# Weight conversion with its first step in an attention PSUM bank, its checks in later blocks, and q in hp's bank for block 0

## The chip, the cores and the metric

One core of one Trainium2 chip runs the whole program. The metric is the time of one execution on the device in microseconds (us); for the kernel before it is the median of three runs. Engine names as in the profile: PE is TensorE, PEld its weight load, DVE VectorE, ACT ScalarE, POOL GpSimd, SP SyncE, whose queue issues the DMAs here.

## The reference

All inputs are float64. First a recurrent attention over 768 time steps for 4 x 8 heads of width 48, then two feed-forward layers over the 3072 tokens that result (384 wide):

```python
for t in range(S):                                   # attention, state is D x D
    cur = einsum('bhd,bhe->bhde', u[None] * kt, vt)
    y[:, :, t] = einsum('bhd,bhde->bhe', rt, state + cur)
    state = wt[:, :, :, None] * state + einsum('bhd,bhe->bhde', kt, vt)
x = y.transpose(0, 2, 1, 3).reshape(B * S, H * D)
h = x @ w_in;  x = (h - tanh(h)) @ w_out             # first layer, d_ff 2048
h = x @ w_in2; e = exp(h - max(h)); sm = e / (sum(e) + 1e-9)
out = (layernorm(h * sm) * g_ln) @ w_out2            # second layer, d_ff 1024
```

## The kernel before

The attention works in chunks of 128 time steps: 24 units (4 batches of 6 chunks), each in stages att_pre and att_0 to att_4. A unit's r, k, w and v come by four DMAs of 192 KB (att_load); TensorE transposes them (tp), VectorE forms running products of w (inc, L201) and decayed keys (kh, L214 and L215), TensorE multiplies qk, kt, ds and y. Stages of unit u need the state st of unit u-1 (L254, L255). The result y goes as a pair of tiles, a rounded value and its remainder, into xs, six small DMAs from x3 included.

The first layer (part1, part2) works on blocks of 512 tokens, six blocks, each of 16 steps m over d_ff. In a step part1 multiplies hp (9 matmuls of 128 x 512, since both operands are split in a rounded part and a remainder), then t = hp squared (ScalarE, L315), y = hp * t (VectorE, L316), q (ScalarE, L317), y = (q + const) * y (VectorE, L319), a range check of t (ScalarE, L320), and g in two parts on GpSimd: rounding (L321) and remainder (L322). part2 adds g of two steps ago into the three x2p banks (9 matmuls). Block i needs the units 4i to 4i+3; four units of the next block are worked in between the steps. The second layer's h and o matmuls follow, after block 5.

The weights arrive as float64 bit patterns: a raw tile of 128 x 2 x 384 pairs of words holds a pair, 128 columns of w_in and 128 rows of w_out (768 KB). convert makes float32 of it: ScalarE scales the low words (L118); VectorE shifts and masks the high words (L119, a one-input operation on 768 elements), ors in the sign (L120) and adds the low part (L121); ScalarE rounds (L124), GpSimd takes the remainder (L125); then ScalarE checks the high words with two passes (L127 and L128, in place, so the raw tile comes free only behind them). There are 16 pairs of the first layer (raw_a, conv_a, due before step m of block 0) and 8 of the second (raw_b, conv_b, in block 5). Raw tiles have two buffers, cv_x too.

PSUM: three banks x2p, two banks "h" for hp, three banks "a" for the attention's tiles (in units 0 to 3 the h and x2p banks serve too). A pool's buffers are handed out in the order in which the code asks for them. The code is written in the order of the loops, and a scheduler then sets the order of each engine's instructions by its own estimates; within an engine they run in that order. fast_path puts two conv_a between the first four units, and conv_a of pair s + 2 into step s:

```python
first += [(2.0 * m, lambda m: K.conv_a(cv, cvr, m), m) for m in range(early)]
...
        if 0 <= s < NM - early:
            K.conv_a(cv, cvr, s + early)
```

Of the kernel before, what the change touches and what calls it, by code (L numbers as in the profile page):

```python
# [55 lines left out]
class Kern:  # L56
# [49 lines left out]
    def like(self, a, out):  # L106
        return a if len(out.shape) == 2 else a.rearrange("p (j f) -> p j f", j=out.shape[1])

    def convert(self, pool, raw, hi, lo, col, scale=None):

        nc, v = self.nc, self.nc.vector
        flat = raw.rearrange("p i f two -> p (i f) two")
        H_, L_ = flat[:, :, 1], flat[:, :, 0]
        x = pool.tile([128, 2 * DM], U32, tag="cv_x", name="cv_x")
        xf = x.bitcast(F32)
        nc.scalar.activation(L_, L_, AF.Copy, scale=2.0**-29)  # L118
        v.tensor_scalar(x, H_, 3, 0x3FFFFFF8, ALU.logical_shift_left, ALU.bitwise_and)  # L119
        v.scalar_tensor_tensor(x, H_, 0xC0000000, x, ALU.bitwise_and, ALU.bitwise_or)  # L120
        v.tensor_tensor(x, x, L_, ALU.add)  # L121
        if scale is not None:
            nc.scalar.activation(xf[:, DM:], xf[:, DM:], AF.Copy, scale=scale)
        nc.scalar.copy(hi, xf)  # L124
        nc.gpsimd.tensor_tensor(lo, xf, hi, ALU.subtract)  # L125
        Hf = H_.bitcast(F32)
        nc.scalar.activation(Hf, Hf, AF.Square)  # L127
        nc.scalar.activation(Hf, Hf, AF.Relu, bias=self.c_flag, scale=-1.0, accum_out=self.flags[:, col:col + 1])  # L128


    def att_setup(self, att, xp0, xp1):
# [164 lines left out]
        return raw  # L296

    def conv_a(self, pool, rpool, m):
        raw = rpool.tile([128, 2, DM, 2], U32, tag="raw", name="raw_a")
        self.load_w1(raw[:, 0], m)  # L300
        self.load_w2(raw[:, 1], m)
        self.convert(pool, raw, self.wa[:, 0, m], self.wa[:, 1, m], 2 * NU + NB * NM + m)

    def part1(self, i, m):
        nc, v, g = self.nc, self.nc.vector, self.nc.gpsimd
        hp = self.ps_h.tile([128, BLK], F32, tag="h", name="hp")
        xs = self.xs[i % 2]
        seq = [(a, b, j) for j in range(KM) for a, b in ((1, 0), (0, 1), (0, 0))]
        for n, (a, b, j) in enumerate(seq):
            self.mm(hp, self.wa[:, a, m, j * 128:(j + 1) * 128], xs[:, b, j], start=n == 0, stop=n == len(seq) - 1)  # L310
        t = self.gp.tile([128, BLK], F32, tag="t", name="t")
        q = self.gp.tile([128, BLK], F32, tag="q", name="q")
        y = self.gp.tile([128, BLK], F32, tag="y", name="y")
        gs = self.gs.tile([128, 2, BLK], F32R, tag="g", name="g")
        nc.scalar.activation(t, hp, AF.Square)  # L315
        v.tensor_tensor(y, hp, t, ALU.mult)  # L316
        nc.scalar.activation(q, t, AF.Square, bias=self.c_fsb, scale=F_S)  # L317
        col = 2 * NU + i * NM + m
        v.scalar_tensor_tensor(y, q, F_E, y, ALU.add, ALU.mult)  # L319
        nc.scalar.activation(q, t, AF.Relu, bias=self.c_t2, accum_out=self.flags[:, col:col + 1])  # L320
        g.tensor_scalar(gs[:, 0], y, 1.0, 1.0, ALU.mult, ALU.mult)  # L321
        g.tensor_tensor(gs[:, 1], y, gs[:, 0], ALU.subtract)  # L322
        return gs

# [36 lines left out]
        return raw  # L361

    def conv_b(self, pool, rpool, k):
        raw = rpool.tile([128, 2, DM, 2], U32, tag="raw", name="raw_b")
        self.load_w3(raw[:, 0], k)
        self.load_w4(raw[:, 1], k)
        self.convert(pool, raw, self.wb[:, 0, k], self.wb[:, 1, k], 2 * NU + NB * NM + NM + k, self.gl[:, k:k + 1])
# [92 lines left out]
def fast_path(tc, K, const):  # L460
    nc = tc.nc
# [280 lines left out]
```

## Time and profile before

| what | value |
|---|---|
| runs of the kernel before | 842.88, 843.4, 844.35 us; median 843.4 |
| profiled execution | 843.12 us |
| its span, first to last instruction | 841.3 us |
| mean granted TensorE clock | 0.972 |
| busy, share of the span | PE 92%, PEld 77%, DVE 65%, ACT 58%, POOL 48% |
| DMA | 55.43 MB, 66 GB/s in the mean |

The span falls into the start (attention units 0 to 3 and the first conversions, up to the first hp matmul at 79.3 us), block 0 (up to about 193 us), blocks 1 to 4, block 5 with the second layer's conversions (from about 526 us), and the second layer (from 614 us). Shares of busy time are means over these; a stage has to be read by itself.

### The profile page before, as it was taken

To read this page: it belongs to the slowest core of one execution; us is meant where nothing else is said; L and a number is where in the kernel's file an instruction comes from. 1 tells how busy PE (TensorE), PEld (TensorE's weight loads), DVE (VectorE), ACT (ScalarE), POOL (GpSimd) and SP (SyncE) were. 2 spreads that over 40 slices of the span, in tenths; PEclk is the share of its full clock that TensorE was granted. 3 is DMA by queue.
4 is the path that set the end of the run, shared out by engine and by line. 5 is a ranking of instruction groups with operands and counts; after the bars stand their busy time and mean duration, and the time that the engine had idled before them with its cause. 6 is when DMAs were issued, how large, how long until landed. Compare 5 with 4: busy or idle time off the path is not lost.

```text
span 841.3 us, 13250 instructions
## 1 busy us (share of the span) xinstructions
PE 773.4 (92%) x4706; PEld 646.9 (77%) x4706; DVE 550.4 (65%) x949; ACT 486.0 (58%) x912; POOL 406.4 (48%) x376
## 2 busy tenths in 40 slices
PE   5556598899999999999999999989989999999996
PEld 3545476688888888888888888767869999999996
DVE  4968798967655566555556555585376667666763
ACT  4655778856555655565556555687545454444442
POOL 4645487866556555556565554668412111111110
PEclk9876899999999999999999999999999999999999
DMA  9976547443222222232132000230011111111100
GB/s 162 172 164 131 124 117 155 105 93 81 43 44 43 71 51 36 41 80 44 33 51 71 16 6 24 80 113 10 1 56 48 39 47 38 48 48 39 48 29 33
DMA packets 137484, 55.43 MB, mean 66 GB/s; under 512 B 105792, under 2 KB 132032, under 8 KB 137408
## 3 DMA queue, kind: packets, MB, share of 16 engines
q1 hardware_dynamic: 137408, 54.49, 28.7%
q8 instruction: 39, 0.64, 0.3%
q14 instruction: 37, 0.30, 0.1%
HBM read 42.67 MB, written 9.44 MB: 62 GB/s over the span
## 4 chain that ended last, share of the span: by engine, by line
PE 77%; DVE 7%; DMA 5%; issue 3%; SPq 3%; ACT 3%; POOL 2%; DVEq 0%; ACTq 0%; POOLq 0%
PE x2p L329 20%; PE hp L310 20%; PE o L431 12%; PE h L386 11%; PE tp L192 3%; PE qk L228 3%; PE tt L420 2%; DMA raw_a<-in_moe_w_out_dram 2%; PE y L270 2%; PE y L267 2%; DVE cv_x L119 1%; SPq L161 1%; PE kt L234 1%; DVE cv_x L120 1%; DVE y L319 1%
## 5 line engine op out<-in xcount | busy, mean ns | idle before, releaser
L329 PE MATMUL x2p<-g,wa 128*128 128x512 f32 x864 | 223.8, 399 | 10.9 <-POOL g L322 9.5
L310 PE MATMUL hp<-xs,wa 128*128 128x512 f32 x864 | 226.1, 402 | 4.4 <-DVE y L316 4.4
L329 PEld LDWEIGHTS x2p<-g,wa 128*128 128x128 f32 x864 | 159.7, 189 | 48.0 <-POOL g L322 12.7
L310 PEld LDWEIGHTS hp<-xs,wa 128*128 128x128 f32 x864 | 163.4, 192 | 42.4 <-DVE y L316 7.1
L321 POOL TENSOR_SCALAR g<-y 128x512 fp32r<-128x512 f32 x96 | 71.1, 740 | 132.4 <-DVE y L319 122.7
L322 POOL TENSOR_TENSOR g<-y,g 128x512 fp32r<-128x512 f32 x96 | 131.1, 1366 | 7.3
L316 DVE TENSOR_TENSOR y<-hp,t 128x512 f32<-128x512 f32 x96 | 66.0, 689 | 93.1 <-ACT t L315 77.1
L320 ACT ACTIVATE q<-t,cst 128x512 f32<-128x512 f32 x96 | 69.6, 725 | 78.6 <-DVE y L319 78.4
L431 PE MATMUL o<-wb,ts 128*128 128x384 f32 x576 | 110.1, 341 | 2.1 <-DVE st L400 1.1
L386 PE MATMUL h<-wb,x2s 128*128 128x512 f32 x432 | 103.9, 392 | 1.6 <-DVE so L406 1.4
L431 PEld LDWEIGHTS o<-wb,ts 128*128 128x128 f32 x576 | 100.4, 188 | 4.3 <-DVE st L400 1.3
L386 PEld LDWEIGHTS h<-wb,x2s 128*128 128x128 f32 x432 | 80.6, 188 | 18.5 <-issue 1.8
L319 DVE SCALAR_TENSOR_TENSOR y<-q,y 128x512 f32<-128x512 f32 x96 | 87.8, 915 | 9.7 <-ACT q L317 4.4
L315 ACT ACTIVATE t<-hp 128x512 f32<-128x512 f32 x96 | 56.9, 593 | 58.7 <-PE hp L310 58.7
L411 POOL TENSOR_TENSOR st<-st,cst 128x1 f32<-128x1 f32 x24 | 13.8, 576 | 136.7 <-DVE st L410 136.7
L317 ACT ACTIVATE q<-t,cst 128x512 f32<-128x512 f32 x96 | 69.4, 723 | 2.4
L192 PE MATMUL tp<-ident,rkw 128*128 128x128 f32 x264 | 41.7, 293 | 13.8 <-DMA rkw<-in_w_dram 5.7
L409 ACT ACTIVATE e<-so 128x1024 f32<-128x1024 f32 x24 | 25.5, 1061 | 49.0 <-DVE so L408 47.2
L192 PEld LDWEIGHTS tp<-ident,rkw 128*128 128x128 f32 x264 | 31.5, 147 | 21.8 <-issue 17.7
L402 DVE TENSOR_REDUCE part<-e 128x32 f32<-128x1024 f32 x24 | 29.3, 1220 | 28.4 <-ACT e L401 28.4
L228 PE MATMUL qk<-rh,kh 48*128 48x128 f32 x384 | 31.6, 310 | 17.6 <-DVE kh L215 17.6
L399 DVE TENSOR_REDUCE st<-h 128x1 f32<-128x1024 f32 x24 | 29.4, 1224 | 27.7 <-PE h L386 26.2
(116 smaller groups left out, 1164.3 us busy)
## 6 DMA issues: line engine op xcount, KB each, us to landing
raw_a<-in_moe_w_out_dram SPq DMA_DIRECT2D x16, 384.0 KB, 4.5
rkw<-in_w_dram SPq DMA_DIRECT2D x24, 192.0 KB, 3.7
rkw<-in_r_dram SPq DMA_DIRECT2D x24, 192.0 KB, 4.1
rkw<-in_k_dram SPq DMA_DIRECT2D x24, 192.0 KB, 3.5
vt<-in_v_dram SPq DMA_DIRECT2D x24, 192.0 KB, 3.7
raw_a<-in_moe_w_in_dram SPq DMA_DIRECT2D x32, 144.0 KB, 3.6
x2d<-x2o SPq DMA_DIRECT2D x18, 256.0 KB, 2.3
x2s<-x2d SPq DMA_DIRECT2D x24, 192.0 KB, 2.5
```

Of the source, the lines that this page charges most:

```text
L192: self.nc.tensor.transpose(p[:, j], self.rkw[u % 2][:, i, 2 * j:2 * j + 2, :], self.ident)
L310: self.mm(hp, self.wa[:, a, m, j * 128:(j + 1) * 128], xs[:, b, j], start=n == 0, stop=n == len(seq) - 1)
L315: nc.scalar.activation(t, hp, AF.Square)
L316: v.tensor_tensor(y, hp, t, ALU.mult)
L317: nc.scalar.activation(q, t, AF.Square, bias=self.c_fsb, scale=F_S)
L319: v.scalar_tensor_tensor(y, q, F_E, y, ALU.add, ALU.mult)
L320: nc.scalar.activation(q, t, AF.Relu, bias=self.c_t2, accum_out=self.flags[:, col:col + 1])
L321: g.tensor_scalar(gs[:, 0], y, 1.0, 1.0, ALU.mult, ALU.mult)
L322: g.tensor_tensor(gs[:, 1], y, gs[:, 0], ALU.subtract)
L329: self.mm(self.x2p[d], self.wa[:, a, m, sl], gs[:, b], start=m == 0 and n == 0, stop=m == NM - 1 and n == 2)
L386: self.mm(p[:, f], xs[:, a, j], self.wb[:, b, 4 * f:4 * f + 4, j * 128:(j + 1) * 128], start=q == 0, stop=q == 8)
L431: self.mm(p, ts[:, a, k], self.wb[:, b, k, DM:], start=q == 0, stop=q == 3 * NM2 - 1)
```

## The change

convert takes its first two VectorE steps in two halves of 384 elements. For the first layer's pairs each half's shifted words go into a tile cv_a from the attention's "a" banks instead of into cv_x; for the second layer's they stay in cv_x. The two checking passes leave convert. They become check_pair: the raw pair is loaded a second time and checked, each behind the last ScalarE instruction of a step, 24 of them at 3 of 7 steps from step 16 (start of block 1) to step 70 (in block 4). In block 0 q is written into hp's own bank, and g's rounding runs on ScalarE instead of GpSimd.

```diff
-    def convert(self, pool, raw, hi, lo, col, scale=None):
+    def convert(self, pool, raw, hi, lo, scale=None, bank=None):
...
         nc.scalar.activation(L_, L_, AF.Copy, scale=2.0**-29)
-        v.tensor_scalar(x, H_, 3, 0x3FFFFFF8, ALU.logical_shift_left, ALU.bitwise_and)
-        v.scalar_tensor_tensor(x, H_, 0xC0000000, x, ALU.bitwise_and, ALU.bitwise_or)
+        for i in range(2):
+            s = slice(i * DM, (i + 1) * DM)
+            if bank is None:
+                a = x[:, s]
+            else:
+                a = bank.tile([128, 4, C], F32, tag="a", name="cv_a").rearrange("p j t -> p (j t)")[:, 0:DM].bitcast(U32)
+            v.tensor_scalar(a, H_[:, s], 3, 0x3FFFFFF8, ALU.logical_shift_left, ALU.bitwise_and)
+            v.scalar_tensor_tensor(x[:, s], H_[:, s], 0xC0000000, a, ALU.bitwise_and, ALU.bitwise_or)
         v.tensor_tensor(x, x, L_, ALU.add)
...
-        Hf = H_.bitcast(F32)
-        nc.scalar.activation(Hf, Hf, AF.Square)
-        nc.scalar.activation(Hf, Hf, AF.Relu, bias=self.c_flag, scale=-1.0, accum_out=self.flags[:, col:col + 1])
+
+    def check(self, raw, col):
+        nc = self.nc
+        H_ = raw.rearrange("p i f two -> p (i f) two")[:, :, 1].bitcast(F32)
+        nc.scalar.activation(H_, H_, AF.Square)
+        nc.scalar.activation(H_, H_, AF.Relu, bias=self.c_flag, scale=-1.0, accum_out=self.flags[:, col:col + 1])
+
+    def check_pair(self, rpool, n):
+
+        raw = self.load_pair(rpool, n)
+        with self.tc.issue_after(self.last_act.ins):
+            self.check(raw, 2 * NU + NB * NM + n)
...
-        self.convert(pool, raw, self.wa[:, 0, m], self.wa[:, 1, m], 2 * NU + NB * NM + m)
+        raw = self.load_pair(rpool, m)
+        self.convert(pool, raw, self.wa[:, 0, m], self.wa[:, 1, m], bank=self.ps_a)
...
-        nc.scalar.activation(q, t, AF.Square, bias=self.c_fsb, scale=F_S)
+        p = hp if i == 0 else q
+        nc.scalar.activation(p, t, AF.Square, bias=self.c_fsb, scale=F_S)
         col = 2 * NU + i * NM + m
-        v.scalar_tensor_tensor(y, q, F_E, y, ALU.add, ALU.mult)
-        nc.scalar.activation(q, t, AF.Relu, bias=self.c_t2, accum_out=self.flags[:, col:col + 1])
-        g.tensor_scalar(gs[:, 0], y, 1.0, 1.0, ALU.mult, ALU.mult)
+        v.scalar_tensor_tensor(y, p, F_E, y, ALU.add, ALU.mult)
+        self.last_act = nc.scalar.activation(q, t, AF.Relu, bias=self.c_t2, accum_out=self.flags[:, col:col + 1])
+        if i == 0:
+            nc.scalar.copy(gs[:, 0], y)
+        else:
+            g.tensor_scalar(gs[:, 0], y, 1.0, 1.0, ALU.mult, ALU.mult)
...
+        n, due = divmod(3 * (s - NM), 7)
+        if 0 <= n < NM + NM2 and due < 3:
+            K.check_pair(cvr, n)
```

load_pair is the loading that conv_a and conv_b did before. In the changed file the lines have other numbers: L118, L119, L120 and L121 are L118, L125, L126 and L127, L124 is L130; L214 and L215 are L240 and L241; L315, L316, L317, L319 and L320 are L339, L340, L342, L344 and L345; g's rounding on ScalarE is L347; the check is L136 and L137.

VectorE in the start, from the keys of attention unit 2 (kh_129) on, before:

```order
L214 TENSOR_TENSOR kh_129<-kh_129,tp 112x512
L121 ISA cv_x<-raw_a,cv_x 128x1536
L215 SCALAR_TENSOR_TENSOR kh_129<-inv,kh_129 112x512
L119 TENSOR_SCALAR cv_x<-raw_a 128x768
L120 SCALAR_TENSOR_TENSOR cv_x<-raw_a,cv_x 128x768
L121 ISA cv_x<-raw_a,cv_x 128x1536
L230 COPY_PREDICATED aq<-mask,qk 128x512 x2
L177 TENSOR_REDUCE dg_137<-inv 128x4x2
```

and the same place now (L227 and L232 form inc and rh, L300 and L301 the x of the unit, L256 is L230):

```order
L240 TENSOR_TENSOR kh_129<-kh_129,tp 112x512
L241 SCALAR_TENSOR_TENSOR kh_129<-inv,kh_129 112x512
L232 TENSOR_TENSOR rh_128<-x2p_118,inc_126 112x512
L300 TENSOR_TENSOR xs_139<-y,xs_139 112x3x128
L301 TENSOR_TENSOR x_138<-y,x_138 112x128
L256 COPY_PREDICATED aq<-mask,qk 128x512 x2
L203 TENSOR_REDUCE dg_137<-inv 128x4x2
```

The conversions between the units' instructions are gone: pair 0 and pair 1 stand ahead of this place, and the conversion of pair 2 begins only behind unit 4's keys and its qk.

VectorE in block 0, the third and fourth step of part1, before:

```order
L206 TENSOR_TENSOR rh_128<-tp,inc_126 112x512
L120 SCALAR_TENSOR_TENSOR cv_x<-raw_a,cv_x 128x768
L121 ISA cv_x<-raw_a,cv_x 128x1536
L316 TENSOR_TENSOR y<-hp,t 128x512 x2
L214 TENSOR_TENSOR kh_130<-kh_130,tp 112x512
L319 SCALAR_TENSOR_TENSOR y<-q,y 128x512
L215 SCALAR_TENSOR_TENSOR kh_130<-inv,kh_130 112x512
```

and now, at the same steps:

```order
L240 TENSOR_TENSOR kh_130<-kh_130,tp 112x512
L126 SCALAR_TENSOR_TENSOR cv_x<-raw,cv_a 128x384
L340 TENSOR_TENSOR y<-hp,t 128x512
L241 SCALAR_TENSOR_TENSOR kh_130<-inv,kh_130 112x512
L344 SCALAR_TENSOR_TENSOR y<-hp,y 128x512
L127 ISA cv_x<-raw,cv_x 128x1536
L344 SCALAR_TENSOR_TENSOR y<-hp,y 128x512
L125 TENSOR_SCALAR cv_a<-raw 128x384
```

The halves of a conversion stand between the steps' instructions, and L344 reads hp's bank where L319 read q.

ScalarE in block 1, two steps, before:

```order
L171 ACTIVATE inv,flags<-rkw_120,cst 128x384
L173 ACTIVATE inv,flags<-rkw_120,cst 128x384
L315 ACTIVATE t<-hp 128x512
L317 ACTIVATE q<-t,cst 128x512
L320 ACTIVATE q,flags<-t,cst 128x512
L235 COPY kn<-kt 128x448
```

and now, at one of the checks:

```order
L199 ACTIVATE inv,flags<-rkw_119,cst 128x384
L345 ACTIVATE q,flags<-t,cst 128x512
L136 ACTIVATE raw<-raw 128x768
L339 ACTIVATE t<-hp 128x512
L137 ACTIVATE raw,flags<-raw,cst 128x768
L342 ACTIVATE q<-t,cst 128x512
```

The two passes of the check stand behind a step's last instruction and between t and q of the next step.

## Rows read from the trace of the kernel before

**Rows 1.** The page's 40 slices: busy tenths of TensorE, and of the DMA engines.

```profile
PE   5556598899999999999999999989989999999996
...
DMA  9976547443222222232132000230011111111100
```

**Rows 2.** Windows: stretch and its us, busy us of PE, PEld, DVE, ACT, POOL, clock, DMA share, GB/s.

```profile
0.00:79.30 79.30, 41.83 (x336) 33.58 (x337) 57.05 (x105) 46.37 (x85) 41.88 (x44) 0.82 0.88 159
79.30:96.70 17.40, 12.41 (x84) 10.06 (x83) 10.94 (x15) 10.73 (x18) 5.86 (x5) 0.79 0.55 148
96.70:182.10 85.40, 75.29 (x447) 58.51 (x447) 76.10 (x103) 68.10 (x131) 68.42 (x50) 0.97 0.52 120
194.00:526.00 332.00, 332.00 (x2253) 272.03 (x2252) 196.91 (x353) 190.94 (x391) 191.77 (x183) 1.00 0.23 47
526.00:590.00 64.00, 58.82 (x243) 45.68 (x242) 42.04 (x42) 48.15 (x88) 46.71 (x36) 0.97 0.20 67
```

**Rows 3.** The chain that ended last, 0 to 181 us: start, us, what.

```profile
48.87 4.79 DMA raw_a<-in_moe_w_out_dram
```

**Rows 4.** Groups of VectorE, 0 to 79.3 us: busy us, mean ns, idle before, releasers.

```profile
L121 DVE CUSTOM_DVE_ANT_0 cv_x<-raw_a,cv_x 128x1536 uint16<-128x1536 uint16 x7 | 8.4, 1201 | 0.4
L120 DVE SCALAR_TENSOR_TENSOR cv_x<-raw_a,cv_x 128x768 uint32<-128x768 uint32 x8 | 8.3, 1040 | 0.2
...
L119 DVE TENSOR_SCALAR cv_x<-raw_a 128x768 uint32<-128x768 uint32 x8 | 5.1, 637 | 11.8 <-DMA raw_a<-in_moe_w_out_dram 7.6 <-DMA xs<-x 4.2
```

**Rows 5.** Timeline, single instructions of VectorE, TensorE, ScalarE: start, us, what, idle before.

```profile
17.71 0.58 DVE L119 TENSOR_SCALAR cv_x<-raw_a 128x768 uint32<-128x768 uint32 x1 [3.35 <-DMA raw_a<-in_moe_w_out_dram]
...
75.88 0.68 DVE L215 SCALAR_TENSOR_TENSOR kh<-inv,kh 112x512 f32<-112x512 f32 x1
...
79.31 4.89 PE L310 MATMUL hp<-xs,wa 128*128 128x512 f32 x16
...
87.69 0.56 DVE L119 TENSOR_SCALAR cv_x<-raw_a 128x768 uint32<-128x768 uint32 x1 [5.23 <-DMA raw_a<-in_moe_w_in_dram]
...
96.74 0.68 DVE L316 TENSOR_TENSOR y<-hp,t 128x512 f32<-128x512 f32 x1
...
182.13 0.69 DVE L316 TENSOR_TENSOR y<-hp,t 128x512 f32<-128x512 f32 x1 [0.77 <-ACT t L315]
...
193.68 0.60 ACT L334 ACTIVATE x2o<-x2p 128x512 f32<-128x512 f32 x1
```

**Rows 6.** Groups of VectorE, 96.7 to 182.1 us, columns as in Rows 4.

```profile
L319 DVE SCALAR_TENSOR_TENSOR y<-q,y 128x512 f32<-128x512 f32 x15 | 18.1, 1206 | 2.3 <-ACT q L317 2.2
L316 DVE TENSOR_TENSOR y<-hp,t 128x512 f32<-128x512 f32 x14 | 9.5, 680 | 1.8 <-ACT t L315 1.3 <-POOL g L322 0.6
L121 DVE CUSTOM_DVE_ANT_0 cv_x<-raw_a,cv_x 128x1536 uint16<-128x1536 uint16 x7 | 9.2, 1318 | 0.7 <-ACT t L315 0.5
L120 DVE SCALAR_TENSOR_TENSOR cv_x<-raw_a,cv_x 128x768 uint32<-128x768 uint32 x6 | 8.1, 1344 | 0.1
...
L119 DVE TENSOR_SCALAR cv_x<-raw_a 128x768 uint32<-128x768 uint32 x6 | 5.2, 858 | 2.5 <-DMA xs<-x 2.2 <-DMA raw_a<-in_moe_w_out_dram 0.4
...
L274 DVE TENSOR_TENSOR xs<-y,xs 112x384 fp32r<-112x384 f32 x4 | 2.2, 542 | 0.0
```

**Rows 7.** The line L119 by itself, whole span: shortest, median, longest in ns.

```profile
L119 DVE TENSOR_SCALAR cv_x<-raw_a x16: 540/560/1391, 17.7 to 142.7; 128x768 uint32<-128x768 uint32 x16
```

**Rows 8.** Groups of ScalarE, 96.7 to 182.1 us, columns as in Rows 4.

```profile
L128 ACT ACTIVATE raw_a<-raw_a,cst 128x768 f32<-128x768 f32 x7 | 7.1, 1009 | 0.0
...
L127 ACT ACTIVATE raw_a<-raw_a 128x768 f32<-128x768 f32 x6 | 5.4, 906 | 1.8 <-DVE cv_x L120 1.8
```

**Rows 9.** Groups of GpSimd, 96.7 to 182.1 us, columns as in Rows 4.

```profile
L321 POOL TENSOR_SCALAR g<-y 128x512 fp32r<-128x512 f32 x15 | 14.1, 939 | 9.7 <-DVE y L319 9.7
```

**Rows 10.** Groups of TensorE, 526 to 614 us, columns as in Rows 4.

```profile
L329 PE MATMUL x2p<-g,wa 128*128 128x512 f32 x171 | 42.7, 394 | 2.0 <-POOL g L322 1.2 <-ACT x2o L334 0.8
L310 PE MATMUL hp<-xs,wa 128*128 128x512 f32 x153 | 39.9, 406 | 3.2 <-DVE y L316 3.2
```

More of the change, by code (lines that the diff above doesn't have):

```diff
@@ L125, in convert, with load_pair @@
         nc.gpsimd.tensor_tensor(lo, xf, hi, ALU.subtract)
-        Hf = H_.bitcast(F32)
-        nc.scalar.activation(Hf, Hf, AF.Square)
-        nc.scalar.activation(Hf, Hf, AF.Relu, bias=self.c_flag, scale=-1.0, accum_out=self.flags[:, col:col + 1])
+    def check(self, raw, col):
[7 more added lines that the diff above has]
+            self.check(raw, 2 * NU + NB * NM + n)
+    def load_pair(self, rpool, n):
+        raw = rpool.tile([128, 2, DM, 2], U32, tag="raw", name="raw")
+        if n < NM:
+            self.load_w1(raw[:, 0], n)
+            self.load_w2(raw[:, 1], n)
+        else:
+            self.load_w3(raw[:, 0], n - NM)
+            self.load_w4(raw[:, 1], n - NM)
+        return raw
     def att_setup(self, att, xp0, xp1):
@@ L298, in conv_a @@
     def conv_a(self, pool, rpool, m):
-        raw = rpool.tile([128, 2, DM, 2], U32, tag="raw", name="raw_a")
-        self.load_w1(raw[:, 0], m)
-        self.load_w2(raw[:, 1], m)
-        self.convert(pool, raw, self.wa[:, 0, m], self.wa[:, 1, m], 2 * NU + NB * NM + m)
+        raw = self.load_pair(rpool, m)
+        self.convert(pool, raw, self.wa[:, 0, m], self.wa[:, 1, m], bank=self.ps_a)
     def part1(self, i, m):
@@ L316, in part1 @@
         v.tensor_tensor(y, hp, t, ALU.mult)
-        nc.scalar.activation(q, t, AF.Square, bias=self.c_fsb, scale=F_S)
+        p = hp if i == 0 else q
+        nc.scalar.activation(p, t, AF.Square, bias=self.c_fsb, scale=F_S)
         col = 2 * NU + i * NM + m
-        v.scalar_tensor_tensor(y, q, F_E, y, ALU.add, ALU.mult)
-        nc.scalar.activation(q, t, AF.Relu, bias=self.c_t2, accum_out=self.flags[:, col:col + 1])
-        g.tensor_scalar(gs[:, 0], y, 1.0, 1.0, ALU.mult, ALU.mult)
+        v.scalar_tensor_tensor(y, p, F_E, y, ALU.add, ALU.mult)
+        self.last_act = nc.scalar.activation(q, t, AF.Relu, bias=self.c_t2, accum_out=self.flags[:, col:col + 1])
+        if i == 0:
+            nc.scalar.copy(gs[:, 0], y)
+        else:
+            g.tensor_scalar(gs[:, 0], y, 1.0, 1.0, ALU.mult, ALU.mult)
         g.tensor_tensor(gs[:, 1], y, gs[:, 0], ALU.subtract)
@@ L363, in conv_b @@
     def conv_b(self, pool, rpool, k):
[L364 to L367, printed above, removed]
+        raw = self.load_pair(rpool, NM + k)
+        self.convert(pool, raw, self.wb[:, 0, k], self.wb[:, 1, k], self.gl[:, k:k + 1])
     def load_x2(self, n):
```

## Prediction

> **What bounds the kernel now.** I read the slices of the page first: the TensorE digit is low over the first seven slices, dips a little in the slices from 526 to 590 us, and is 9 nearly everywhere else [rows 1]. The windows by stage say the same in us [rows 2]: from 194 to 526 us TensorE is busy 332.0 of 332 us at full clock, so nothing that another engine saves there can shorten the kernel. Three places can give something: the start up to the first hp matmul (41.83 us busy of 79.3, granted clock 0.82, DMA engines 88% busy), token block 0 behind it, and the last block with its conversions (58.82 of 64).
>
> In the start the chain that ended last goes again and again through the arrival of a raw weight tile and then through conversion steps on VectorE [rows 3]. VectorE's groups for the start show why [rows 4]: eight conversions were begun there, each of three instructions of 637, 1040 and 1201 ns, 2.88 us together, and the first of the three waited 11.8 us in all with everything of the attention queued behind it. The marks that I use [rows 5]: VectorE finishes the keys of attention unit 4 (L215) at 75.88 + 0.68; the first hp matmul is at 79.31; the second L316 at 96.74; the sixteenth L316 at 182.13; the first x2o of block 0, which follows its last x2p, at 193.68.
>
> Between the second and the sixteenth L316 (85.4 us) VectorE is busy 76.1 and TensorE 75.3 [rows 2], so VectorE is what the rest waits for, and its instructions are stretched: L319 takes 1206 ns in the mean there, L316, which reads as many elements but one operand from PSUM, 680 [rows 6].
>
> **The change, part by part.** The sum is made against the profiled execution, 843.12 us (span 841.3 and 1.8 around it); the median of three runs is 843.4.
>
> *Conversions leave the start.* The new tiles cv_a rotate through the three "a" banks of the attention in program order, so the conversion of pair 2 and later can no longer run ahead of the attention; VectorE's rows above show two conversions up to the attention of unit 4 instead of seven. Saved on VectorE, which carries the chain to L215 of unit 4: 5 x 2.88 = 14.4 us. Of the 11.8 us of waiting, 3.35 is the first conversion's own and stays [rows 5]; the other 8.4 goes. Added: two conversions in halves, 0.5 us each (below), 1.0; and the ds matmuls of unit 4 now stand ahead of hp on TensorE, behind kt and its copy, 1.5 us, an estimate from the 2.08 us and 1 us steps of that chain at the low clock. First hp: 79.3 - 14.4 - 8.4 + 1.0 + 1.5 = 59.0, **-20.3 us**. Ends: 67 if the attention's own latencies fill all 8.4 us, 55 if some of the stretching of the attention's VectorE work goes too. DMA does not forbid it: 20 attention loads of 192 KB and 4 raw pairs of 768 KB are 6.9 MB, 43 us at the 159 GB/s of that stretch [rows 2].
>
> *From the first hp to the second L316*, 17.4 us now. VectorE waits 5.23 us there for a raw tile [rows 5]; pairs 2 and 3 will have been loaded during the start. 17.4 - 5.2 = 12.2; I take 11, as the stretched L255 goes partly: **-6.4 us**. Ends 8 and 17.
>
> *Second to sixteenth L316.* By the two orders VectorE has 12 conversions between these marks instead of 8 (six of raw_a in [rows 6], two of raw_b). One costs 858 + 1344 + 1318 = 3.52 us now [rows 6]. The halves: a 384-wide VectorE instruction with a PSUM operand, L274, takes 542 ns [rows 6]; four of them are 2.17. Bounds of one half: 270 (half of the fastest L119, 540 for 768 [rows 7]) and 680 (the 512-wide L316); I take 542, the same width and memory. The add (L121) stays at 1.2: 3.4 a conversion. 12 x 3.4 - 8 x 3.52 = +12.6. q in hp's bank: 15 L319 fall from 1206 to the 680 of L316, -7.9; end 0 if the stretching has another cause. Sum **+4.6 us**, 90 instead of 85.4, with the 9.3 us of idle kept. ScalarE and GpSimd stay cover: ScalarE (68.1 busy) loses the checks, about 8 x 1.92 (L127 and L128 [rows 8]) = 15, and gets 14 roundings of some 0.6 (the 512-wide copy out of PSUM [rows 5]) = 8.4; GpSimd (68.4) loses the 14.1 us of L321 [rows 9] and gets four more subtractions. If that cover were gone, each rounding would add its 0.6. hp's bank is now free only after L319's successor instead of after L316, one ScalarE pass of 0.7 to 1.6 us and 0.7 on VectorE later; two banks at 6 us a step leave room, so I cost it at nothing; without that room it costs up to 2 us on a step. Ends of the whole stretch: -5 (GpSimd's lighter load lets VectorE's other stretched work, L121 and L215, shorten) and +14 (each of the 24 halves waits 0.4 us for its bank).
>
> The row of L119 says that this instruction is quick for its width: 540 ns for 768 elements at best, against 1040 and more for L120. [...] No row of before shows a VectorE instruction that writes PSUM.
>
> *The checks*, 24 pairs of ScalarE passes, move into blocks 1 to 4, each behind the last ScalarE instruction of a step, with the weights loaded a second time: 18.4 MB more and 96 DMAs more on SP. A raw load on SP waits for the check two before it; behind it stand the attention loads, which are two units ahead. ScalarE is busy 190.9 of 332 us there and gets 24 x 1.92 = 46; DMA's share is 0.23 [rows 2]. Each check can hold up the next t or kn by 2 us; TensorE gets hp two steps ahead. **+1 us**; ends 0 and 7.
>
> *Last block*: TensorE waits 3.2 us for L316 and 2.0 ahead of x2p [rows 10], and ScalarE, 48.2 busy of 64, loses six checks, 12 us. **-2.5 us**; ends -5 and +1 (two more VectorE instructions in each of eight conversions).
>
> Sum: -20.3 - 6.4 + 4.6 + 1 - 2.5 = -23.6, 819.5; with the 0.3 of the median, **820 us**.
>
> **The rivals.**
> - *The start is held by the attention's own chain and its loads*, not by the conversions: DMA at 0.88 speaks for it, the 8.4 us of waiting for raw tiles against it. First hp at 67: 828.
> - *L319 is long for another reason than its two SBUF operands.* L316 in the same stretch never lengthens, which speaks against; then q in PSUM saves nothing, 820 + 7.9 = 828. [...]
> - *The checks reach TensorE*: one ScalarE pass of 1 us between kt and kn or ahead of t, 24 times, with TensorE at 100%: up to 24 us, 820 + 12 = 832 at half of that. For it: TensorE runs in order; against: ScalarE is idle 141 us there.
> - *Slower: the banks.* Three "a" banks serve eight attention tiles a unit and now eight halves in the same four steps. If a half waits for a bank that TensorE's attention tile holds, VectorE stands with all behind it, 24 times. It decides from (23.6 + 1.7) / 24 = 1.05 us a half; at 1.3 us the time is 820 + 31 = 851. Now VectorE waits almost nowhere for TensorE in that stretch, and the halves of a pair stand close together in its order.
>
> **How the numbers follow.** Forecast 60%, held start 16%, L319 6%, checks 8%, banks 10%. A measurement of this kernel tells 0.2% (1.7 us) from no change. Faster: the first four and nothing of the last, less some of the checks' upper end, 0.87; same 0.04; slower 0.09. Independent ends of the terms combine to about -11 and +15 around 820; reaching toward the held start and the checks gives 807 to 838.
>
> **What would show it.** In the profile after: first hp at 55 to 67 (not 79); two conversions ahead of unit 4's keys; halves near 0.54 us and L319's successor near 0.68 in block 0; the sixteenth L316 near 160; first x2o near 171; TensorE without idle in blocks 1 to 4. The prediction is wrong if VectorE shows waits for TensorE's attention tiles ahead of the halves in block 0, if TensorE has holes behind the checks, or if the first hp stays past 70.

## The result, and the profile after

The changed kernel takes **833.6 us** (median of four runs, 832.52 to 837.36) against 843.7 for the kernel before in the same comparison: a ratio of 0.9891, interval 0.9871 to 0.9911. It is faster by 1.1%, clear of noise, as forecast, and inside the range (807 to 838), but by 10 us and not by 23. The profiled execution has a span of 831.7 us, 9.6 less than that of before.

The marks of the prediction, in the changed kernel. First the timeline's single instructions (start, us, what, idle before):

```profile
61.62 0.69 DVE L241 SCALAR_TENSOR_TENSOR kh<-inv,kh 112x512 f32<-112x512 f32 x1
...
66.78 1.65 PE L334 MATMUL hp<-xs,wa 128*128 128x512 f32 x3
...
75.19 0.69 DVE L340 TENSOR_TENSOR y<-hp,t 128x512 f32<-128x512 f32 x1 [0.79 <-ACT t L339]
...
167.97 0.69 DVE L340 TENSOR_TENSOR y<-hp,t 128x512 f32<-128x512 f32 x1 [0.38 <-ACT t L339]
...
179.68 1.08 ACT L362 ACTIVATE x2o<-x2p 128x512 f32<-128x512 f32 x2
...
440.04 1.55 ACT L362 ACTIVATE x2o<-x2p 128x512 f32<-128x512 f32 x3
...
602.64 1.08 ACT L362 ACTIVATE x2o<-x2p 128x512 f32<-128x512 f32 x2
```

The last two are the first x2o of blocks 3 and 5; in the kernel before they stand at 452.74 and 612.24. Stretch by stretch, against [rows 2, 5]:

| stretch | before | after | measured | forecast |
|---|---|---|---|---|
| start, to the first hp | 79.31 | 66.78 | -12.5 | -20.3 |
| first hp to second L340 | 17.43 | 8.41 | -9.0 | -6.4 |
| second to sixteenth L340 | 85.39 | 92.78 | +7.4 | +4.6 |
| sixteenth L340 to first x2o of block 0 | 11.55 | 11.71 | +0.2 | 0 |
| x2o of block 0 to x2o of block 3 | 259.06 | 260.36 | +1.3 | +1 |
| x2o of block 3 to x2o of block 5 | 159.50 | 162.60 | +3.1 | -2.5 |
| rest | 229.06 | 229.06 | 0.0 | 0 |

The windows of the changed kernel (stretch and its us, busy us of PE, PEld, DVE, ACT, POOL, clock, DMA share, GB/s), to be read against [rows 2]:

```profile
0.00:66.80 66.80, 42.06 (x353) 33.62 (x353) 43.53 (x96) 26.45 (x55) 30.34 (x40) 0.92 0.86 142
...
75.20:168.00 92.80, 83.03 (x457) 64.27 (x455) 78.78 (x139) 67.67 (x128) 59.35 (x41) 0.93 0.62 146
...
180.00:512.00 332.00, 331.73 (x2246) 270.76 (x2245) 201.79 (x360) 230.27 (x464) 188.26 (x181) 1.00 0.45 108
440.04:602.64 162.60, 155.36 (x848) 123.30 (x847) 103.28 (x153) 98.51 (x190) 92.63 (x82) 0.99 0.21 64
```

Blocks 1 to 4 stay full: TensorE is busy 331.73 of 332 us, although DMA's share went from 0.23 to 0.45 and ScalarE from 191 to 230 us. In block 0 VectorE is busy 78.8 of 92.8 us and TensorE 83.0: VectorE has 14 us to spare there now, and it is no longer what the rest waits for (the runs on q and on the rounding, below, bear that out). The groups of VectorE in that window (busy us, mean ns, idle before and releasers), beside [rows 6]:

```profile
L127 DVE CUSTOM_DVE_ANT_0 cv_x<-raw,cv_x 128x1536 uint16<-128x1536 uint16 x12 | 14.9, 1240 | 0.1
L125 DVE TENSOR_SCALAR cv_a<-raw 128x384 uint32<-128x384 uint32 x24 | 13.1, 554 | 2.0 <-DMA raw<-in_moe_w_in_dram 1.7
L126 DVE SCALAR_TENSOR_TENSOR cv_x<-raw,cv_a 128x384 uint32<-128x384 uint32 x24 | 12.9, 543 | 0.1
L340 DVE TENSOR_TENSOR y<-hp,t 128x512 f32<-128x512 f32 x15 | 10.3, 684 | 6.7 <-ACT t L339 6.7
L344 DVE SCALAR_TENSOR_TENSOR y<-hp,y 128x512 f32<-128x512 f32 x15 | 10.2, 682 | 1.0 <-ACT hp L342 0.9
```

Durations came out as written: a half 0.55 us, a conversion (13.1 + 12.9 + 14.9) / 12 = 3.41, L344 at 0.68. And no half waited for a bank: the 2.0 us that L125 waits for go to its raw tile (1.7).

In the last block TensorE's waits, and VectorE's conversions of the second layer's pairs, now in halves in SBUF (440 to 604 us):

```profile
PE x2p L357 <- POOL g L350: 4.4, 3, 3.2
PE x2p L357 <- ACT x2o L362: 1.0, 1, 1.0
```

```profile
L126 DVE SCALAR_TENSOR_TENSOR cv_x<-raw,cv_x 128x384 uint32<-128x384 uint32 x16 | 16.3, 1051 | 0.0
L125 DVE TENSOR_SCALAR cv_x<-raw 128x384 uint32<-128x384 uint32 x16 | 12.4, 803 | 5.2 <-POOL wb L131 4.0 <-DMA raw<-in_moe_w_in_dram 1.2
L127 DVE CUSTOM_DVE_ANT_0 cv_x<-raw,cv_x 128x1536 uint16<-128x1536 uint16 x8 | 9.1, 1132 | 0.7
```

That is (16.3 + 12.4 + 9.1) / 8 = 4.7 us a conversion; whole steps took 3.8 in the kernel before. Six of the eight stand behind 520 us, as six did before; the other two stand at 463 to 476 us, in block 4.

### The profile page after: what moved, and what is told of

It is laid out like the page before. It is cut to its first block, busy times and chain, and to the rows that moved or that the text cites. A ratio compares the mean times of both kernels' runs of the same rounds, so it can differ in the third digit from the quotient of the medians.

```text
span 831.7 us, 13450 instructions
## 1 busy us (share of the span) xinstructions
PE 779.4 (94%) x4706; PEld 649.1 (78%) x4706; DVE 548.6 (66%) x997; ACT 490.5 (59%) x928; POOL 377.2 (45%) x360
## 3 DMA queue, kind: packets, MB, share of 16 engines
HBM read 61.54 MB, written 9.44 MB: 85 GB/s over the span
## 4 chain that ended last, share of the span: by engine, by line
PE 75%; DVE 11%; DMA 4%; issue 2%; POOL 2%; ACT 2%; SPq 2%; DVEq 0%; ACTq 0%; POOLq 0%
PE hp L334 19%; PE x2p L357 18%; PE o L457 12%; PE h L412 11%; PE qk L254 3%; PE tp L218 3%; DVE cv_x L126 2%; PE tt L446 2%; DVE cv_x L127 2%; PE y L296 2%; PE y L293 2%; DMA raw<-in_moe_w_out_dram 1%; DVE cv_x L125 1%; DMA raw<-in_moe_w_in_dram 1%; PE kt L260 1%
## 5 line engine op out<-in xcount | busy, mean ns | idle before, releaser
L357 PE MATMUL x2p<-g,wa 128*128 128x512 f32 x864 | 226.4, 401 | 9.0 <-POOL g L350 4.6
L350 POOL TENSOR_TENSOR g<-y,g 128x512 fp32r<-128x512 f32 x96 | 129.3, 1347 | 17.4 <-ACT g L347 9.7
L340 DVE TENSOR_TENSOR y<-hp,t 128x512 f32<-128x512 f32 x96 | 66.2, 689 | 106.6 <-ACT t L339 103.6
L345 ACT ACTIVATE q<-t,cst 128x512 f32<-128x512 f32 x96 | 69.5, 724 | 68.1 <-DVE y L344 67.8
L349 POOL TENSOR_SCALAR g<-y 128x512 fp32r<-128x512 f32 x80 | 53.9, 674 | 114.8 <-DVE y L344 111.4
L339 ACT ACTIVATE t<-hp 128x512 f32<-128x512 f32 x96 | 56.6, 591 | 44.8 <-PE hp L334 44.6
L437 POOL TENSOR_TENSOR st<-st,cst 128x1 f32<-128x1 f32 x24 | 13.5, 563 | 136.2 <-DVE st L436 134.8
L344 DVE SCALAR_TENSOR_TENSOR y<-q,y 128x512 f32<-128x512 f32 x80 | 65.4, 818 | 10.6 <-ACT q L342 5.6
L342 ACT ACTIVATE q<-t,cst 128x512 f32<-128x512 f32 x80 | 57.7, 722 | 2.0
L402 POOL TENSOR_TENSOR x2s<-x2s 128x384 fp32r<-128x384 f32 x24 | 24.4, 1018 | 48.3 <-ACT x2s L401 40.0
L131 POOL TENSOR_TENSOR wa<-cv_x,wa 128x768 fp32r<-128x768 f32 x16 | 29.4, 1838 | 35.3 <-ACT wa L130 35.3
```

The source lines that it names most:

```text
L342: nc.scalar.activation(p, t, AF.Square, bias=self.c_fsb, scale=F_S)
L344: v.scalar_tensor_tensor(y, p, F_E, y, ALU.add, ALU.mult)
L345: self.last_act = nc.scalar.activation(q, t, AF.Relu, bias=self.c_t2, accum_out=self.flags[:, col:col + 1])
L357: self.mm(self.x2p[d], self.wa[:, a, m, sl], gs[:, b], start=m == 0 and n == 0, stop=m == NM - 1 and n == 2)
```

## The experiments

Unless said otherwise each is the changed kernel with one edit; compare its time with 833.6.

### What keeps the conversions out of the start

```diff
-        self.convert(pool, raw, self.wa[:, 0, m], self.wa[:, 1, m], bank=self.ps_a)
+        self.convert(pool, raw, self.wa[:, 0, m], self.wa[:, 1, m], bank=None)
```

> The changed kernel, with the shifted words of the first layer's pairs in cv_x (SBUF) instead of an attention PSUM bank; halves, late checks, q in hp's bank and ScalarE's rounding stay. Theory (the bank's place in the rotation is what keeps conversions out of the start): conversions run ahead again, first hp at 76 to 82 us instead of 66.8, steps of the conversion stretched (L126 0.8 us or more instead of 0.54), time 838 to 846 us against 833.6. Rival (the late checks and loads freed the start, not the bank): first hp stays within 2 us of 66.8 and the time within 3 us of 833.6.

It took 851.3 us, 1.009 of the kernel before (1.0056 to 1.0123) and above the 838 to 846 expected, with the first hp at 82.26. Two rows, of the timeline and of VectorE's groups up to there:

```profile
82.26 2.05 PE L334 MATMUL hp<-xs,wa 128*128 128x512 f32 x4
```

```profile
L126 DVE SCALAR_TENSOR_TENSOR cv_x<-raw,cv_x 128x384 uint32<-128x384 uint32 x16 | 14.1, 882 | 0.3
```

Eight conversions run ahead again. The bank is what holds them; late checks free nothing in the start.

The opposite test is the kernel before with the bank alone: halves through a PSUM bank for the first layer's pairs, checks inside the conversion, q in its own tile, rounding on GpSimd, whole steps for the second layer.

> The kernel before with one part of the change alone: the first layer's conversions in halves through an attention PSUM bank. The checks stand in the conversion again, q of block 0 in its own tile, rounding on GpSimd, the second layer's conversions in whole steps. Theory (the gain is the start, and the start is the bank's order; the other parts move nothing): first hp at 66 to 70 us, time 832 to 836 us. Rival (the checks in the conversion hold the raw tiles and ScalarE, so that the bank alone doesn't free the start): first hp at 72 or later, time 838 to 844.

836.2 us (ratio 0.9905, 0.9883 to 0.9927), first hp at 66.82. The bank alone gives the start and most of the whole gain: 1.2 us are missing by the ratios, 2.5 by the medians, and its interval overlaps that of the full change.

Then the order without the bank: conversions in whole SBUF steps, the one of pair s + 2 put by hand behind ScalarE's last instruction of step s - 1.

```diff
+        with self.tc.issue_after(behind.ins) if behind else nullcontext():
+            self.convert(pool, raw, self.wa[:, 0, m], self.wa[:, 1, m])
...
+            K.conv_a(cv, cvr, s + early, K.prev if s else K.last_act)
```

> The changed kernel with all conversions in whole steps in SBUF, held back in the order by hand: the conversion of pair s + 2 is put behind ScalarE's last instruction of step s - 1. It is the order without the bank. Theory (the start's gain is order alone; PSUM only makes the steps quick): first hp at 66 to 70 us against 82.3 where the same conversions were free to run ahead, time 834 to 840, some us above the changed kernel since L125 and L126 are stretched in block 0. Rival (the bank's short unstretched steps made the start quick): first hp at 73 or later, time above 842.

The first hp came at 69.67, so order alone frees the start; but the time is 842.2 us (0.997), longer than the theory had it. The 9.6 us won there were gone by the first x2o of block 0, at 193.36 against 193.68 before. VectorE between the first and the sixteenth y of that run:

```profile
L126 DVE SCALAR_TENSOR_TENSOR cv_x<-raw,cv_x 128x768 uint32<-128x768 uint32 x12 | 18.3, 1528 | 0.1
L125 DVE TENSOR_SCALAR cv_x<-raw 128x768 uint32<-128x768 uint32 x12 | 13.2, 1098 | 4.6 <-DMA raw<-in_moe_w_out_dram 3.9 <-issue 0.8
```

L125 and L126 cost 31.5 us for twelve conversions here and 26.0 through the bank, and TensorE's idle time from the first hp to the x2o of block 1 is 18.9 us instead of 10.0. From the first hp to 182 us TensorE waits 13.5 us for VectorE's y, kh and inc, in the changed kernel 4.0. So the bank does two things: it holds the conversions back, and it makes their first two steps short. That the short steps alone account for the lost 9.6 us isn't shown, since the order set by hand differs from the bank's in block 0 too.

### What the start is made of

Weights of pairs 0 and 1 as zeros, not loaded and not converted:

```diff
+    nc.gpsimd.memset(K.wa[:, :, 0:2].bitcast(F32), 0.0)
...
-    first += [(2.0 * m, lambda m: K.conv_a(cv, cvr, m), m) for m in range(early)]
```

> The changed kernel without loading and converting weight pairs 0 and 1 (their weights are zeros here, so two of sixteen terms of the first layer are left out); pairs 2 and 3 are loaded as soon as their tiles are free. It shows the start with attention alone. Theory (the attention's own chain from unit to unit is the floor of the start; two waits for raw tiles, 5.1 us, are all that conversions add now): first hp at 59 to 62 us instead of 66.8. Rival A (DMA's bandwidth holds the start, 0.86 busy): 1.5 of 9.4 MB less gives 11 us, first hp at 55 to 57. Rival B (VectorE's work holds it): 6.3 us of conversions and the 5.1 us of waits go, 55.

The first hp came at 61.54. With no conversion in the start at all, VectorE is busy 35.22 of these 61.5 us; its longest waits up to the first hp and just behind it (us in total, times, longest):

```profile
DVE aq L256 <- PE qk L254: 7.5, 4, 2.3
DVE inc L227 <- PE tp L218: 5.7, 1, 5.7
DVE xs L300 <- ACT x L299: 5.2, 2, 3.1
DVE dg L203 <- POOL inv L202: 2.3, 4, 0.8
```

The same pairs loaded, not converted:

> The changed kernel with pairs 0 and 1 loaded as before but not converted (zeros as their weights, two of sixteen terms of the first layer left out). It keeps the DMA traffic of the start and takes away the conversion work. Theory (attention's chain): as without the loads, first hp at 59 to 62. Rival A (DMA's bandwidth): within 1.5 us of 66.8. Rival B (VectorE's work): 55 to 57.

63.56, later than the theory's 59 to 62 and 3.2 before the changed kernel. Of the 5.2 us that pairs 0 and 1 cost, 2.0 are their loads and 3.2 their conversion, as far as one execution each can tell: over the runs here that leave the start's code alone the first hp lies between 65.76 and 67.04. To separate the attention's loads from its chain, v of units 1 to 5 was not loaded:

> The changed kernel without the loads of v for attention units 1 to 5 (they use unit 0's v, so the attention's results of these units are others); 0.98 of the 9.4 MB that the start moves are gone, the order of work is the same. Rival (the loads' bandwidth holds the start, DMA 0.86 busy at 142 GB/s): 6.9 us less, first hp at 59 to 61. Theory (the chain from unit to unit holds it): first hp at 65 to 67.

The first hp stayed at 66.80 with five loads of 192 KB less, so the bandwidth of the DMA engines doesn't hold the start. That the loads play no part doesn't follow. In the run without pairs 0 and 1, the chain that ended last goes through loads for its first 27 us: through SyncE, which issues them one behind the other (in the changed kernel's trace the four of one unit at 5.10, 6.24, 7.42 and 8.51 us, 1.04 to 1.14 us each), and then through the landing of a k tile and a w tile (start, us, what):

```profile
16.57 5.27 DMA rkw<-in_k_dram
21.91 5.30 DMA rkw<-in_w_dram
...
27.35 1.09 PE x2p L218 x4
```

TensorE waits 4.66 us for that w tile. Only behind it does the chain go from unit to unit, through TensorE, VectorE, ScalarE and GpSimd. Shortening the start was also not worth its length: without pairs 0 and 1 the first hp is 5.2 us earlier, the x2o of block 1 (264.35 against 266.65) 2.3.

### Checks, q and rounding in block 0

Without the 24 moved checks and their loads:

> The changed kernel without the 24 moved checks and their second loads (the range check of the weights is left out, its flags are zero). Theory (blocks 1 to 4 have room for them; the trace gives 1.3 us between the first x2o of block 0 and that of block 4): time 831.5 to 833.5 us against 833.6. Rival (18.4 MB of loads and 46 us of ScalarE slow TensorE's operands and the last block's first raw loads): below 830 us.

836.2 us (0.9905, 0.9878 to 0.9931), no faster, and above what either side had expected. (What the expectation calls block 4's x2o is block 3's.) From the x2o of block 1 to that of block 3 it takes 173.6 us, the changed kernel 173.4. The checks cost TensorE nothing there.

q of block 0 in its own tile (`p = q`):

> The changed kernel with q of block 0 in its own SBUF tile again. Theory (VectorE is what block 0 waits for, and L344 with two SBUF operands is stretched): L344 of block 0 goes from 682 to about 1150 ns, some 7 us more on VectorE, the stretch from the second to the sixteenth L340 from 92.8 to 97 to 100, time 838 to 841 us. Rival (block 0 is now set by TensorE at the granted clock and by the raw loads): L344 as long, but the time within 1.5 us of 833.6.

```profile
L344 DVE SCALAR_TENSOR_TENSOR y<-q,y 128x512 f32<-128x512 f32 x15 | 14.8, 992 | 0.7 <-ACT q L342 0.7
```

L344 takes 992 ns with two operands in SBUF and 682 with one in PSUM, so the operand's place costs 4.7 us over fifteen steps. Yet the time is 834.4 us (0.9884, 0.9861 to 0.9908), the same as with the change. The theory that VectorE bounds block 0 after the change fell.

The rounding of block 0 on GpSimd:

> The changed kernel with g's rounding of block 0 on GpSimd again. Theory (GpSimd has 59 of 93 us busy in block 0, so it has room for 14 us, but it stretches VectorE's SBUF instructions when it works): L127 and L241 get longer, time 834 to 838 us. Rival (ScalarE's pass lies on g's way and GpSimd would do as well): time 832 to 834. A third way: GpSimd's remainder of the weights and g queue behind each other, TensorE waits for g over 6 us in block 0, time over 838.

833.5 us (0.9877, 0.9844 to 0.991): the rival, no difference. L127 went from 1240 to 1303 ns, and L241 did not get longer (906 ns against 1479).

### The last block

Whole steps again for the second layer's pairs:

```diff
-        for i in range(2):
-            s = slice(i * DM, (i + 1) * DM)
+        for i in range(1 if bank is None else 2):
+            s = slice(0, 2 * DM) if bank is None else slice(i * DM, (i + 1) * DM)
```

> The changed kernel, with the second layer's conversions in whole steps of 768 again (one L125 and one L126 in SBUF), all else as changed. Theory (the halves in SBUF are what made the last block 3 us longer, since each of the extra instructions is stretched beside GpSimd): VectorE's conversion of a wb pair falls from 4.7 to about 3.8 us, TensorE's wait for g (L350) in the last block goes from 4.4 to below 2, time 829.5 to 831.5 us. Rival (GpSimd's remainder of the weights and the moved checks set the last block): L350's wait stays above 3.5 us and the time within 1 us of 833.6.

831.8 us (0.9862, 0.9829 to 0.9894), an interval that overlaps the changed kernel's. Between the x2o of blocks 3 and 5 it needs what the kernel before needed; the wait for L350 fell from 4.4 to 0.6 us, though TensorE waits 4.0 for L340 now:

```profile
441.46:600.95 159.49, 153.64 (x847) 123.61 (x846) 98.69 (x137) 99.11 (x189) 96.36 (x83) 0.99 0.21 65
```

The run with the bank alone still has the checks in these conversions, and takes 159.63 there:

```profile
443.70:603.33 159.63, 154.34 (x847) 123.65 (x846) 91.11 (x131) 99.71 (x192) 96.25 (x83) 0.99 0.14 40
```

So taking the checks out of the last block was worth 0.1 us; six conversions stand behind 520 us in either run. The stretch tells the forms apart better than the time does: over all the runs here with q and the rounding of the last block left alone, it takes 162.3 to 164.0 us with halves in SBUF, 159.5 to 159.6 with whole steps, and 158.0 to 158.5 in the runs below that use PSUM.

The conversions themselves, with whole steps:

```profile
L127 DVE CUSTOM_DVE_ANT_0 cv_x<-raw,cv_x 128x1536 uint16<-128x1536 uint16 x8 | 14.7, 1832 | 0.7
L126 DVE SCALAR_TENSOR_TENSOR cv_x<-raw,cv_x 128x768 uint32<-128x768 uint32 x8 | 9.3, 1162 | 0.2
L125 DVE TENSOR_SCALAR cv_x<-raw 128x768 uint32<-128x768 uint32 x8 | 8.6, 1071 | 6.6 <-POOL wb L131 5.1 <-DMA raw<-in_moe_w_out_dram 1.4
```

They take (14.7 + 9.3 + 8.6) / 8 = 4.1 us each, not the 3.8 expected: the first two steps are shorter than in halves, but the add behind them (L127) rose from 1132 to 1832 ns. About half of what the two steps gained was lost again there.

The second layer's shifted words in PSUM as well, in a two-bank tile of that layer's pool:

```diff
+            a = self.ps_r.tile([128, 2, 512], F32, tag="h2", name="cv_b")[:, :, 0:DM].bitcast(U32)
...
```

> The changed kernel with the shifted words of the second layer's pairs, too, in PSUM: one two-bank tile of the second layer's pool, unused until that layer, written and read in whole steps of 768. Theory (in the last block, too, the stretch comes from two SBUF operands beside GpSimd): both steps of a conversion at 1.0 to 1.1 us without stretching, time 829 to 831 us, below the 831.8 of whole steps in SBUF. Rival (GpSimd's remainder of the weights sets the pace of the last block): steps short, but the time 831 to 833.

829.6 us (0.9821, 0.9798 to 0.9845), as the theory had it. The stretch takes 158.5 us. Its VectorE steps (L122, L123 and L130 are here what L125, L126 and L127 are in the changed kernel):

```profile
L122 DVE TENSOR_SCALAR cv_b<-raw 128x768 uint32<-128x768 uint32 x8 | 7.6, 954 | 2.8 <-DMA raw<-in_moe_w_out_dram 2.7
L123 DVE SCALAR_TENSOR_TENSOR cv_x<-raw,cv_b 128x768 uint32<-128x768 uint32 x8 | 7.6, 948 | 0.7 <-POOL wb L134 0.6
...
L130 DVE CUSTOM_DVE_ANT_0 cv_x<-raw,cv_x 128x1536 uint16<-128x1536 uint16 x8 | 13.5, 1684 | 0.3
```

The add, which still has its operands in SBUF, takes 1684 ns.

From there, q in hp's bank and the rounding on ScalarE in the last block too:

> The changed kernel with the second layer's shifted words in PSUM, and in the last block q in hp's bank and g's rounding on ScalarE as in block 0. Theory (VectorE is what the last block waits for at 530 to 560 us, its SBUF instructions stretched beside GpSimd): L344's successor there at 0.68 instead of 0.89 us, TensorE's waits for y and g fall from 4.7 to about 2 us, time 826.5 to 828.5 against 829.55. Rival (hp's bank held longer, or the third ScalarE pass on g's way, costs what VectorE gains): 829 to 832.

834.9 us (0.9901, 0.9867 to 0.9936), slower. The rival, and by more than its 829 to 832. To see which part did it, q alone:

```diff
-        p = hp if i == 0 else q
+        p = hp if i in (0, NB - 1) else q
```

> The kernel with all shifted words in PSUM (829.55 us) and q of the last block in hp's bank, rounding there on GpSimd. Theory (hp's bank is held until VectorE has read q, and in the last block TensorE comes back to it every other step of 4.2 us, with no attention between): TensorE waits 5 us or more for y there, 833 to 836 us. Rival (ScalarE's rounding made it): TensorE waits below 3 us, 827 to 830.

834.0 us (0.9883, 0.9859 to 0.9909). TensorE's wait, and below it the one of the run it started from:

```profile
PE hp L337 <- DVE y L347: 7.6, 2, 6.1
```

```profile
PE hp L337 <- DVE y L343: 3.4, 1, 3.4
```

L347 is the step that reads q, L343 the one that forms y. hp's bank is free a ScalarE pass and a VectorE step later, and in the last block, with no attention between the steps, TensorE stands before it. The longest waits of the two runs end at the same place (532.3 and 533.0 us), so of the 6.1 us some 2.6 are new; a second wait of 1.5 us comes on top.

### A faster version

All shifted words in PSUM, and pair 1 converted later in the start:

```diff
-    first += [(2.0 * m, lambda m: K.conv_a(cv, cvr, m), m) for m in range(early)]
+    first += [(4.2 * m, lambda m: K.conv_a(cv, cvr, m), m) for m in range(early)]
```

> The changed kernel with the second layer's shifted words in PSUM (as the run before that had 829.55 us) and pair 1 converted two unit stages later in the start. Theory (pair 1's raw tile and its GpSimd remainder stand on the attention's chain at 19 to 30 us): first hp at 63 to 65 us instead of 66.2; of it a third to a half is left at the end, 828 to 829.5. Rival (what the start gains, TensorE gives back as idle time and low clock in block 0): first hp earlier, the time 829 to 831.

**824.9 us** (0.9772, 0.9746 to 0.9797), faster than both kernels and below both ranges, and not for the reason given: the first hp is at 66.67. The gain lies behind it, where block 0 has another order. Further in the same direction:

> The kernel with all shifted words in PSUM and pair 1 converted at 6.3 stages instead of 4.2 (824.88 us) or 2 (829.55 us). If the place of pair 1's work in the start itself is what counts, the first hp moves and the time is 823 to 827. If the gain of the run at 4.2 was only another order of block 0 with fewer stretches at the low clock (3.6 us lost against 9.1), the time can land anywhere between 824 and 832, and the first hp stays at 65 to 68.

829.0 us (0.9831, 0.9804 to 0.9858), first hp at 67.75: the second case. From the first hp to the x2o of block 1 (idle time of TensorE, and what the clock took, added up over windows of 2 us as length times one less the granted clock), in the one profiled execution of each kernel:

| kernel | first hp to x2o of block 1 | TensorE idle | lost to the clock |
|---|---|---|---|
| before | 199.8 | 15.1 | 6.1 |
| changed | 199.9 | 10.0 | 8.2 |
| bank alone | 204.2 | 12.4 | 9.5 |
| all in PSUM | 202.4 | 11.7 | 9.1 |
| all in PSUM, pair 1 at 4.2 | 195.6 | 9.1 | 3.6 |
| all in PSUM, pair 1 at 6.3 | 198.7 | 9.0 | 6.2 |
| order alone | 209.0 | 18.9 | 9.0 |

The last column is not the whole explanation of the times. Over the executions of one kernel the mean granted clock of the span moves without them: the fastest execution of the 824.9 us kernel (823.57 us) had 0.975, and one of the 829.6 us kernel had 0.983 and took 829.25 us.

## Why the prediction was right or wrong

**What bounds the kernel: right** for blocks 1 to 4. Of the three places named, the start gained 12.5 us, block 0 with block 1 nothing, and the last block lost 3.1.

**Conversions leave the start: the work right, the waiting wrong.** Two conversions instead of seven, and VectorE's busy time up to the keys of unit 4 fell from 55.0 to 40.4 us, 14.7 where 13.4 were worked out; the ds matmuls ahead of hp cost 1.7, not 1.5. The step that failed is "the other 8.4 goes". VectorE's idle time up to those keys was 21.5 us and is 21.9: the waits for raw tiles fell from 11.5 to 5.5 (4.2 of the 11.5 stand in the profile as a wait for the transfer xs<-x), and waits of the attention took their place. Those of the changed kernel, 0 to 62 us:

```profile
DVE cv_a L125 <- DMA raw<-in_moe_w_in_dram: 5.1, 2, 2.9
DVE dg L203 <- POOL inv L202: 3.2, 3, 2.1
DVE inc L227 <- PE tp L218: 3.2, 2, 2.2
...
DVE aq L256 <- PE qk L254: 2.6, 1, 2.6
```

That is the rival "the start is held by the attention's own chain and its loads", with 67 for the first hp. The forecast of 59 lay below the 61.5 that the start needs with no conversion at all. Of the rival's two halves the runs rule out only bandwidth: in the run with 61.5 the chain goes through the issue and landing of loads up to 27 us and from unit to unit behind that. How much each of the two would give is open. The count of the loads was low as well: 6.9 MB were reckoned, and 9.5 MB had moved by the first hp (142 GB/s over 66.8 us). This term is 7.8 of the 13.6 us between forecast and result.

**Block 0: the durations right, what they are worth wrong.** Twelve conversions of 3.4 us are as forecast. L319's successor fell from 1206 to 682 ns, the 7.9 us of the sum; but with q back in its own tile it takes 992, so q's place saves 4.7 of them, and the rest came with the other edits. The step that failed is that the sum took VectorE's work as time. The two stretches together were forecast at -1.8 and gave -1.6, and even that was handed back: from the first hp to the x2o of block 1 the two kernels need 199.8 and 199.9 us, since TensorE is busy 185 to 190 of them, the stretches at the low clock included. What moved, in the profiled executions, was which holes TensorE has and how long it ran at the low clock behind them. q's place and the rounding's could each be put back at no cost.

**hp's bank at nothing: nearly right in block 0, with the room that was named** (one wait of 2.7 us there). The "up to 2 us on a step" without that room was a little low: 2.6 us more in one wait of the last block.

**Checks: right** (+1.3 for +1), and by the run without them it isn't even theirs: the 1.3 lies in block 1.

**The last block: wrong sign, 5.6 us.** Two steps failed. ScalarE's six checks less were taken as 2.5 us of TensorE's waits, and were worth 0.1: of TensorE's waits there 0.8 us were for ScalarE (x2o) before and 1.0 are now, the others for y of VectorE and g of GpSimd. And "two more VectorE instructions in each of eight conversions", held for at most 1 us, cost 3.1. Per conversion the first two steps took 2 x 0.80 + 2 x 1.05 = 3.7 us in halves, and in whole steps 1.14 + 1.30 = 2.4 in the kernel before and 1.07 + 1.16 = 2.2 in the run that puts them back. Of the difference to the kernel before 0.3 is the shortest case (2 x 347 + 2 x 545 ns against 543 + 944) and the rest stretching: what stands above the shortest is 1.9 us a conversion in halves and 1.0 and 0.7 in whole steps. In the traces of the two kernels this part goes with GpSimd's work. In the changed one the second layer's halves during which no GpSimd instruction ran, five L125 and seven L126, took 347 to 360 and 545 to 549 ns, the other eleven and nine up to 2006 and 2193. In the kernel before, over all its pairs, L119 took 543 to 561 and L120 942 to 960 ns with none beside them, up to 2191 and 1943 with one. For these two steps the price went by the number of instructions and not by their width (1.9 us for four, 1.0 and 0.7 for two). For a whole conversion it did so only in part, as the add shows: 1132 ns behind halves, 1832 behind whole steps. With the shifted words in PSUM the two steps have no such part at all, 947 to 964 and 937 to 956 ns.

**The other rivals.** L319 is long for its two SBUF operands for 0.31 of the 0.52 us that it took over L316's 0.68 (992 and 1206 ns), so that rival fell for the greater part. The slower case, halves that wait for banks, did not occur: no half waited for TensorE.

Left open: why the order with pair 1 at 4.2 is the fastest of them. The scheduler's order changes at many places at once, and no run changed one of them alone.

## What to carry to other kernels

Don't count a wait that is removed from a chain as gained before the next wait in the same stretch has been looked up: take the work away in thought and ask what the remaining chain needs by itself, or measure it with the work left out, as the run with 61.5 us did here. Behind the start, add up the busy time of the engine that ends the stretch before an edit on another engine is priced: 4.7 us of VectorE's work gave under 1 us here, in a stretch that TensorE fills to 92% and more. A bank that rotates in program order was also a brake on the scheduler (first hp at 66.8 us with it, 82.3 without); who moves a tile into a shared pool should read the new order first.

## What the runs showed of the hardware

- **L125 was steady into PSUM and quicker at best into SBUF.** L125 on 384 elements, shortest, median, longest over the whole span of the changed kernel:

```profile
L125 DVE TENSOR_SCALAR cv_a<-raw x32: 536/553/568, 15.9 to 155.5; 128x384 uint32<-128x384 uint32 x32
L125 DVE TENSOR_SCALAR cv_x<-raw x16: 347/599/2006, 463.4 to 556.4; 128x384 uint32<-128x384 uint32 x16
```

Into SBUF it is quicker at best (347 against 536 ns) and took up to 2006; into PSUM it stayed at 536 to 568. Of the 32 into PSUM nineteen had a GpSimd instruction beside them (536 to 568) and thirteen had none (548 to 561); of the 16 into SBUF the five with none took 347 to 360 and the eleven with one 353 to 2006. That GpSimd is the cause was not tested by taking its work away.

- **The clock fell behind a short pause, inside a stretch that looks full.** In the changed kernel TensorE waits 2.37 and 0.54 us at 139 and 141 us, and then nine hp matmuls take 4.21 us, where nine took 2.35 just before; from 143 to 151 us the granted clock is 0.50, the lower of the two levels that this trace shows (0.50 and 1.00). Not every pause did this: behind one of 2.71 us, which ends at 78.1 us, the granted clock stayed at 1.00. The rows at 139 us:

```profile
134.72 2.35 PE L334 MATMUL hp<-xs,wa 128*128 128x512 f32 x9
139.43 0.96 PE L357 MATMUL x2p<-g,wa 128*128 128x512 f32 x3 [2.37 <-ACT g L347]
140.94 1.82 PE L254 MATMUL qk<-rh,kh 48*128 48x128 f32 x8 [0.54 <-DVE kh L241]
142.69 4.21 PE L334 MATMUL hp<-xs,wa 128*128 128x512 f32 x9
```

Windows of 10 us behind it, of the changed kernel and of the one at 824.9 us:

```profile
145.00:155.00 10.00, 10.00 (x50) 7.56 (x49) 6.85 (x13) 6.86 (x11) 7.55 (x5) 0.68 0.35 109
```

```profile
145.00:155.00 10.00, 10.00 (x79) 7.99 (x78) 9.88 (x20) 6.50 (x12) 5.20 (x4) 1.00 0.41 112
```

Both are "busy 10 of 10"; one does 50 matmuls in it, the other 79 (of a somewhat different mix). Between the kernels at 829.6 and 824.9 us the work is the same and only its order differs. In the two profiled executions TensorE's idle time and lost clock up to the x2o of block 1 are 11.7 + 9.1 us against 9.1 + 3.6; whether that difference holds in their other executions was not profiled.
